# Issuing the natural K and V pair loads from GpSimd's software queue instead of SyncE's hardware queue, in an attention backward kernel

## The chip, the cores and the metric

The kernel runs on one core of a Trainium2 chip. The metric is the device time of one execution in microseconds (us). Runs are compared as fast runs of the same rounds on the same chip. "Same" means that the 95% interval of the ratio lies within 2%.

A ring is the list in memory through which one queue hands its transfers to the DMA engines. The engines are named as in the profile: PE (TensorE matmul) and PEld (its weight loads), DVE (VectorE), ACT (ScalarE), POOL (GpSimd) and SP (SyncE, which here only issues DMAs).

## The reference

The reference runs two independent blocks, A and B, of attention against a KV cache, and then takes the gradient of everything. The outputs are the forward result and ten gradients. Cut to what matters:

```python
# per block; B, Sq, D = 8, 96, 640;  H, Sk, Dh = 32, 512, 128;  bfloat16
q = (x @ wq).reshape(B, Sq, H, Dh).transpose(0, 2, 1, 3)
scores = jnp.einsum("bhqd,bhkd->bhqk", q, k_cache) * (Dh ** -0.5)
p = softmax(scores, axis=-1)
o = jnp.einsum("bhqk,bhkd->bhqd", p, v_cache)
out = o.transpose(0, 2, 1, 3).reshape(B, Sq, H * Dh) @ wo
# ... both blocks, then
_out, _vjp = jax.vjp(_f, A_x, A_k_cache, A_v_cache, A_wq, A_wo, B_x, B_k_cache, B_v_cache, B_wq, B_wo)
_grads = _vjp(grad_out)
```

K and V of one head and batch are 512 x 128 values each, 128 KB. Over two blocks, 32 heads and 8 batches that is 134 MB to read for both, and as much again in dK and dV to write.

## The kernel before

One head and batch is one *tick* of about 3.3 us; there are 512 ticks. The stages of a tick are spread over several ticks, so that PE works on different batches at once. The kernel's framework has a scheduler that orders each engine's instructions; what an engine gets is one list, and it works through that list in order.

The parts that matter here. K and V are loaded for two batches at a time (256 KB each, 256 runs of 1 KB), in rotating buffers:

```python
def c_ld(h, b):
    def f():
        K_sb = kvp.tile([128, 2, KC, 128], BF16, name="K_sb", bufs=7)
        V_sb = kvp.tile([128, 2, KC, 128], BF16, name="V_sb", bufs=5)
        nc.sync.dma_start(V_sb[:], vc[b:b + 2, h].rearrange("b (p c) d -> p b c d", c=KC))   # L233
        nc.sync.dma_start(K_sb[:], kc[b:b + 2, h].rearrange("b (p c) d -> p b c d", c=KC))   # L234
        # ... cut: the views are kept for later stages
    return f

def c_vt(h, b):      # V transposed by a DMA, issued on SyncE too
    def f():
        VT = kvp.tile([128, 2 * KC, 128], BF16, name="VT", bufs=4)
        nc.sync.dma_start_transpose(VT[:], CS[(blk, h, b)]["V2"][:].rearrange("p a c d -> p (a c d)"))  # L242
        # ... cut
```

POOL has two compute steps per tick. PE transposes the first one's result, and sums the second one's, later:

```python
# c_s3b: P = E / rowsum
P_sb = wk.tile([Sq, Sk], BF16, name="P_sb", bufs=5)
nc.gpsimd.tensor_scalar(P_sb[:], st["E_sb"][:], st["rinv"][:], 0.0, op0=ALU.mult, op1=ALU.add)   # L296
# c_s45, one tick later: PE transposes P_sb
nc.tensor.transpose(PT_ps[:, c * Sq:(c + 1) * Sq], P_sb[:, c * 128:(c + 1) * 128], ident[0:Sq, 0:Sq])   # L319
# c_s5b: O * dO, which PE sums into dl
nc.gpsimd.tensor_tensor(prod[:], hs["OT_h"][:, tok], hs["dOT_h"][:, tok], op=ALU.mult)   # L348
```

POOL's queue already issues other DMAs. The dK and dV stores stay on SyncE:

```python
nc.gpsimd.dma_start(wo_h[:], wo[h * 128:(h + 1) * 128, :])                 # L166, once a head
nc.gpsimd.dma_start(wq_h[:], wq_v[:, :, h * 128:(h + 1) * 128])            # L169, once a head
nc.gpsimd.dma_start(dwo[h * 128:(h + 1) * 128, :], dwo_sb[:])              # L435, once a head
nc.gpsimd.dma_start(wo_r[:, 0:groups[g], :], wo[...])                      # L463, once a group of heads, 1280 KB
nc.gpsimd.dma_start(tmp[:], src_flat[:, c * 128:(c + 1) * 128]...)         # L109, ld_tmp: block B's inputs, early
(nc.sync if first else nc.gpsimd).dma_start(t_[:], src_flat...)            # L136, x_nat and g_nat: SyncE in block A
nc.sync.dma_start(dv[b, h]..., dV_sb[:])                                   # L339, once a tick
nc.sync.dma_start(dk[b, h]..., dK_sb[:])                                   # L403, once a tick
```

## Time and profile before

| | before |
|---|---|
| time, median of 3 runs (range) | 1765.75 us (1764.09 to 1770.63) |
| span of the profiled run, granted clock | 1761.8 us, 1.0 |
| PE busy | 1727.7 us (98%) |
| POOL busy | 775.8 us (44%) |
| bytes moved, mean rate | 402 MB, 228 GB/s |

These are lines of the profile's page. The first gives the busy time of each engine, its share of the span and its instructions. Then come the DMA queues (q1 is the hardware queue, q0 the software queue; packets, MB, and the share of the sixteen DMA engines' time). Then one group of instructions per line: code line, engine, operation, names and shapes, count, busy time and mean ns of one, and after the second bar the engine's idle time before them with what ended most of it.

```profile
PE 1727.7 (98%) x24696; PEld 1467.1 (83%) x24696; DVE 1407.1 (80%) x3309; ACT 1426.4 (81%) x4041; POOL 775.8 (44%) x1378
...
DMA packets 578815, 402.15 MB, mean 228 GB/s; under 512 B 300512, under 2 KB 564192, under 8 KB 578496
...
q1 hardware_dynamic: 558624, 337.64, 80.0%
q0 software_dynamic: 19872, 60.32, 12.3%
...
L296 POOL TENSOR_SCALAR P_sb<-E_sb,rinv 96x512 bf16<-96x512 bf16 x512 | 352.1, 688 | 788.7 <-DVE rinv L287 785.5
```

PE is busy 98% of the span: it is the bound. POOL has more than half of its time free, and 785.5 us of that is one wait: before P_sb, for the reciprocal rinv that DVE delivers.

The list of waits of the same kernel gives engine, line and what it waited for, then us in total, times, and the longest. First over all engines, then for PE alone:

```profile
engine line waited for: us in total, times, longest us
POOL P_sb L296 <- DVE rinv L287: 785.5, 442, 3.7
```

```profile
PE tp_ps L127 <- DMA x_nat<-in_A_x_dram: 5.9, 1, 5.9
PE tp_ps L127 <- DMA g_nat<-in_grad_out_dram: 5.8, 1, 5.8
PE optp_ps L319 <- POOL P_sb L296: 2.6, 5, 1.2
```

PE waits for x_nat and g_nat at the start, once each. After that almost nothing holds it: POOL's P_sb delayed a transpose five times in 512 ticks. No K, V or VT landing is in PE's list.

Here is POOL's own timeline over two and a half ticks (start, duration, instruction, and in brackets the idle time before it and what ended it):

```profile
304.25 0.69 POOL L296 TENSOR_SCALAR P_sb<-E_sb,rinv 96x512 bf16<-96x512 bf16 x1 [2.43 <-DVE rinv L287]
304.91 0.36 POOL L348 TENSOR_TENSOR prod<-OT_h,dOT_h 128x96 bf16<-128x96 bf16 x1
307.42 0.69 POOL L296 TENSOR_SCALAR P_sb<-E_sb,rinv 96x512 bf16<-96x512 bf16 x1 [2.15 <-DVE rinv L287]
```

In a plain tick POOL works for one microsecond and stands for more than two. A load of 0.7 us fits into such a gap, if it comes at the right moment.

For the latencies that follow I matched every instruction of the trace with the one that uses its result. In this kernel K lands 16.15 us (median; 7.25 at the least) before its first transpose, VT 15.99 us (10.7 at the least) before the matmul dP that reads it, and P_sb ends 1.43 us (median; 1.25 at the fifth percentile) before its transposes start.

### The profile page before, as it was taken

Reading aid. Unit: us, or ns where it says so; the run is one execution under the profiler, and the core shown is the slowest. Engines: PE = TensorE matmul, PEld = TensorE weight load, DVE = VectorE, ACT = ScalarE, POOL = GpSimd, SP = SyncE. Lnnn points to the kernel's source line nnn. Section 1 sums busy time; section 2 is a strip of 40 time slices with the busy share of each in tenths; the row PEclk is TensorE's granted clock in tenths of the full one; section 3 lists DMA queues with packets and bytes.
Section 4 is the critical chain, followed back from the end, with each engine's and each line's share of the span. In section 5 each row is a group of like instructions: output and inputs, shape, how many; then the busy total and the mean of one; then the engine's idle time right before and its main releaser. Section 6 shows DMA issues by size and latency. Waiting matters only on the chain. (4 is left out here: it accounts for less than half of the span.)

```text
span 1761.8 us, 65690 instructions
## 1 busy us (share of the span) xinstructions
PE 1727.7 (98%) x24696; PEld 1467.1 (83%) x24696; DVE 1407.1 (80%) x3309; ACT 1426.4 (81%) x4041; POOL 775.8 (44%) x1378
## 2 busy tenths in 40 slices
PE   6999999999999999999999999999999999999998
PEld 5888888888888888888888888888888888888877
DVE  5888856888778887888878887678887888878884
ACT  4999977998679986798867998789976899768991
POOL 4444433444334443345465444344433444334445
PEclk9999999999999999999999999999999999999999
DMA  9999968999779997799999999789997899979982
GB/s 273 258 238 268 246 193 187 256 253 232 215 190 249 253 239 203 191 258 254 234 251 221 259 249 233 197 206 256 250 222 202 212 251 251 216 201 226 247 205 85
DMA packets 578815, 402.15 MB, mean 228 GB/s; under 512 B 300512, under 2 KB 564192, under 8 KB 578496
## 3 DMA queue, kind: packets, MB, share of 16 engines
q1 hardware_dynamic: 558624, 337.64, 80.0%
q0 software_dynamic: 19872, 60.32, 12.3%
q8 instruction: 193, 3.16, 0.8%
q14 instruction: 126, 1.03, 0.2%
HBM read 171.57 MB, written 159.12 MB: 188 GB/s over the span
## 5 line engine op out<-in xcount | busy, mean ns | idle before, releaser
L296 POOL TENSOR_SCALAR P_sb<-E_sb,rinv 96x512 bf16<-96x512 bf16 x512 | 352.1, 688 | 788.7 <-DVE rinv L287 785.5
L277 ACT ACTIVATE E_sb<-S_ps,negm 96x512 bf16<-96x512 f32 x512 | 348.5, 681 | 245.3 <-DVE negm L267 233.2
L362 DVE SCALAR_TENSOR_TENSOR dS_sb<-dP_ps,dl_ps,P_sb 96x512 bf16<-96x512 f32 x512 | 382.4, 747 | 110.2 <-PE dl_ps L360 106.4
L267 DVE TENSOR_REDUCE negm<-S_ps 96x1 f32<-96x512 f32 x512 | 347.4, 679 | 38.1 <-PE S_ps L265 32.7
L338 ACT ACTIVATE dV_sb<-dV_ps 128x512 bf16<-128x512 f32 x512 | 312.6, 611 | 0.5 <-DMA out_dram<-dV_sb 0.5
L402 ACT ACTIVATE dK_sb<-dK_ps 128x512 bf16<-128x512 f32 x512 | 300.3, 587 | 3.0 <-ACT dV_sb L338 2.0
L325 ACT ACTIVATE PT_sb<-optp_ps 128x384 bf16<-128x384 bf16 x512 | 253.5, 495 | 1.4 <-PE optp_ps L319 1.4
L254 DVE COPY KT<-kT_ps 128x512 bf16<-128x512 bf16 x512 | 212.6, 415 | 44.5 <-PE kT_ps L252 44.3
L336 PE MATMUL dV_ps<-dOnat_h,P_sb 96*128 96x128 bf16 x2048 | 197.9, 219 | 0.0
L252 PE MATMUL kT_ps<-ident,K_sb 128*128 128x128 bf16 x2048 | 197.9, 219 | 0.0
L400 PE MATMUL dK_ps<-Qnat_h,dS_sb 96*128 96x128 bf16 x2048 | 197.9, 219 | 0.0
L348 POOL TENSOR_TENSOR prod<-OT_h,dOT_h 128x96 bf16<-128x96 bf16 x512 | 185.9, 363 | 22.4 <-ACT OT_h L322 17.2
L265 PE MATMUL S_ps<-KT,QT_h 128*96 128x512 bf16 x512 | 193.8, 378 | 1.7 <-DVE KT L254 1.5
L358 PE MATMUL dP_ps<-VT,dOT_h 128*96 128x512 bf16 x512 | 195.2, 381 | 0.0
L385 DVE COPY dST_sb<-dq_dst_ps 128x384 bf16<-128x384 bf16 x512 | 178.0, 348 | 0.9 <-PE dq_dst_ps L383 0.8
L252 PEld LDWEIGHTS <-K_sb 128*128 128x128 bf16 x2048 | 147.2, 98 | 36.6 <-issue 1.6
L319 PE MATMUL optp_ps<-ident,P_sb 96*128 96x96 bf16 x2048 | 171.6, 205 | 2.8 <-POOL P_sb L296 2.6
L383 PE MATMUL dq_dst_ps<-ident,dS_sb 96*128 96x96 bf16 x2048 | 172.1, 206 | 1.6 <-DVE dS_sb L362 1.5
L312 PE MATMUL optp_ps<-PT_sb,V_sb 128*128 128x96 bf16 x2048 | 172.1, 206 | 0.0
L376 PE MATMUL dq_dst_ps<-dST_sb,K_sb 128*128 128x96 bf16 x2048 | 170.8, 206 | 0.3
L451 PE MATMUL dwq_ps<-dQnat,x_nat 128*128 128x128 bf16 x1920 | 143.2, 219 | 4.4
L431 PE MATMUL dwo_ps<-g_nat,Onat 128*128 128x128 bf16 (+1 forms) x768 | 140.5, 299 | 0.1
(82 smaller groups left out, 3698.7 us busy)
## 6 DMA issues: line engine op xcount, KB each, us to landing
out_dram<-dV_sb SPq DMA_DIRECT2D x512, 128.0 KB, 3.4
out_dram<-dK_sb SPq DMA_DIRECT2D x512, 128.0 KB, 3.5
V_sb<-in_A_v_cache_dram SPq DMA_DIRECT2D x128, 256.0 KB, 3.7
K_sb<-in_A_k_cache_dram SPq DMA_DIRECT2D x128, 256.0 KB, 4.0
K_sb<-in_B_k_cache_dram SPq DMA_DIRECT2D x128, 256.0 KB, 4.0
V_sb<-in_B_v_cache_dram SPq DMA_DIRECT2D x128, 256.0 KB, 3.6
out_dram<-dwq_sb POOLq DMA_DIRECT2D x64, 160.0 KB, 4.0
out_dram<-dwo_sb POOLq DMA_DIRECT2D x64, 160.0 KB, 3.9
```

The source lines that it names most:

```text
L252: nc.tensor.transpose(kT_ps[:, c * 128:(c + 1) * 128], st["K_sb"][:, c, :], ident[:])
L254: nc.vector.tensor_copy(KT[:], kT_ps[:])
L267: nc.vector.tensor_reduce(negm[:], S_ps[:], axis=AX.X, op=ALU.max, negate=True)
L277: nc.scalar.activation(E_sb[:], st["S_ps"][:], ACT.Exp, bias=st["negm"][:], scale=1.0, accum_out=rowsum[:])
L296: nc.gpsimd.tensor_scalar(P_sb[:], st["E_sb"][:], st["rinv"][:], 0.0, op0=ALU.mult, op1=ALU.add)
L325: nc.scalar.activation(PT_sb[:], PT_ps, ACT.Identity, scale=1.0)
L336: nc.tensor.matmul(dV_ps[:, c * 128:(c + 1) * 128], P_sb[:, c * 128:(c + 1) * 128], hs["dOnat_h"][:, b * 128:(b + 1) * 128], start=True, s ...
L338: nc.scalar.activation(dV_sb[:], dV_ps[:], ACT.Identity, scale=1.0)
L358: nc.tensor.matmul(dP_ps[:], hs["dOT_h"][:, tok], st["VT"], start=True, stop=True)
L362: nc.vector.scalar_tensor_tensor(dS_sb[:], dP_ps[:], dl_ps[:, 0:1], st["P_sb"][:], op0=ALU.subtract, op1=ALU.mult)
L400: nc.tensor.matmul(dK_ps[:, c * 128:(c + 1) * 128], dS_sb[:, c * 128:(c + 1) * 128], hs["Qnat_h"][:, b * 128:(b + 1) * 128], start=True, s ...
L402: nc.scalar.activation(dK_sb[:], dK_ps[:], ACT.Identity, scale=1.0)
```

## The change

The intent is to take 512 DMA issues off SyncE's queue, which also issues the V transposes and the dK and dV stores, and to put them on POOL's, which has idle time.

```diff
-            nc.sync.dma_start(V_sb[:], vc[b:b + 2, h].rearrange("b (p c) d -> p b c d", c=KC))
-            nc.sync.dma_start(K_sb[:], kc[b:b + 2, h].rearrange("b (p c) d -> p b c d", c=KC))
+            nc.gpsimd.dma_start(V_sb[:], vc[b:b + 2, h].rearrange("b (p c) d -> p b c d", c=KC))
+            nc.gpsimd.dma_start(K_sb[:], kc[b:b + 2, h].rearrange("b (p c) d -> p b c d", c=KC))
```

## The prediction

> **What bounds the kernel.** TensorE. The page has PE busy for 1727.7 of 1761.8 us (98%); most of the idle 30-odd us are two waits at the start (5.9 us for x_nat, 5.8 us for g_nat in the list of waits) and the ends. So freeing the SyncE queue cannot pay: no matmul waits for a K, V or VT landing in steady state. By the trace, matched instruction by instruction, K lands 16 us (median; 7 at worst) before its first transpose, VT 16 us (10.7 at worst) before dP.
>
> **What the change moves.** 512 loads (256 K, 256 V, 256 KB each) leave the SyncE queue, where each issue takes 0.39 us (200 us of 1762), for POOL, where a DMA is counted as work. POOL's own DMAs show the price: wo_h (128 runs of 1280 B) 0.60 us, wq_h (640 runs of 256 B) 0.91 us. A K or V load has 256 runs of 1 KB, so my estimate by interpolation is 0.68 us: 512 x 0.68 = 350 us, POOL 776 -> about 1125 us (64%). POOL has over 980 us of idle, 785 of it before P_sb, waiting for rinv.
>
> The Trainium skill (DMA: Bandwidth & Descriptors, "Issuing engines are not separate DMA queues") says all queues end on the same 16 engines, so I expect no bandwidth gain.
>
> **What lies on the critical path.** Only what delays P_sb (POOL) or prod (POOL), since PE transposes P one tick later. In the trace P_sb ends 1.25 us or more before its transposes in 95% of ticks (median 1.43), prod 1.43 us or more before dl. Loads are issued as soon as their buffer is released (K median 0.06, V 0.33 us after the last reader), each once in two ticks, about 0.8 us (V) and 1.3 us (K) before the next P_sb starts. Hence one load mostly fits in POOL's idle time; a collision costs P_sb at most about 0.7 us of its 1.25. Only double collisions (load plus the 0.91 us dwq or wq DMA) or an order in which POOL stands at the head of its queue waiting for a buffer release would reach PE. I allow 0 to 10 us for that.
>
> The Trainium skill (SBUF — State Buffer, "Who interferes with whom") warns that 2-port VectorE operations block descriptor writing. I expect none of it: here VectorE's large operations read PSUM, and POOL's present DMAs are steady (dwq_sb 0.86/0.92/0.93 us min/median/max).
>
> **Start-up.** g_nat lands at 12.45 us and PE waits for it. The first V and K loads stood behind it in the SyncE ring; now up to 1 MB more is in the other ring and may land before it: 1 MB at the 290 GB/s of the first 30 us is 3.6 us at most. I expect +2 us.
>
> **Sum.** 1765.75 + 2 (start) + 1.5 (collisions) = 1769 us; 8 in 10: 1759 to 1790. Faster over 2%: 0.02; within 2%: 0.86; slower over 2%: 0.12.
>
> **What would show it.** POOL busy 1080-1180 us, 0.6-0.75 us per load; PE busy unchanged within 5 us; the wait of PE/PEld for P_sb, 3.8 us before, below 15; K and VT still landing many us before use; PE's second start-up wait longer by 0 to 4 us.
>
> **What would make it wrong.** A per-load POOL time over 1.2 us; an in-order POOL queue that puts a load waiting for PE ahead of the P_sb that PE needs next (then 0.5 us or more per pair, over 100 us); a changed instruction order on PE.

## The result

| | before | after |
|---|---|---|
| time, median (range) of 4 runs | 1766.74 us (1764.09 to 1770.63) | 1765.84 us (1765.20 to 1766.98) |
| ratio, 95% interval | | 0.9994 (0.9974 to 1.0014): same |
| span of the profiled run, granted clock | 1761.8 us, 1.0 | 1764.3 us, 0.999 |
| after again, other rounds (last experiment) | 1768.16 us (1764.66 to 1771.70, 11 runs) | 1777.19 us (1771.11 to 1781.04, 4 runs), ratio 1.0048 (1.0024 to 1.0072): same |

A ratio here is the mean time of one kernel's fast runs over the mean of the other's in the same rounds, so it is not quite the ratio of the medians. The results were correct in every run told below.

The same lines of the page after the change, with one of the new groups of POOL:

```profile
PE 1721.9 (98%) x24547; PEld 1467.9 (83%) x24696; DVE 1407.6 (80%) x3309; ACT 1429.1 (81%) x4041; POOL 1151.6 (65%) x1890
...
DMA packets 480511, 402.15 MB, mean 228 GB/s; under 512 B 300512, under 2 KB 433120, under 8 KB 480192
...
q1 hardware_dynamic: 419360, 203.39, 54.6%
q0 software_dynamic: 60832, 194.57, 38.6%
...
L296 POOL TENSOR_SCALAR P_sb<-E_sb,rinv 96x512 bf16<-96x512 bf16 x512 | 356.5, 696 | 109.3 <-DVE rinv L287 77.8
...
L233 POOL DMA_DIRECT2D V_sb<-in_A_v_cache_dram x128 | 96.1, 751 | 106.5 <-PE optp_ps L319 105.7
```

POOL became 376 us busier, and the span did not follow. Its wait before P_sb for rinv fell from 785.5 to 77.8 us. The issue of one load costs POOL 0.75 us (0.70 to 0.795 over all 512). The bytes moved from q1 to q0: 134 MB, in 139264 packets fewer on q1 and 40960 more on q0. The Trainium skill ("DMA: Bandwidth & Descriptors", "Issuing engines are not separate DMA queues") says that DMAs of all issuing engines run on the same sixteen DMA engines, and that a second issuer saves only issue time. The equal mean rate of 228 GB/s is no test of that, since the same bytes in the same time give the same rate; that the two queues do share the engines is shown by the landings at the start, in experiments 7 to 10. (PE's count is lower after the change because 149 matmul records are missing from that trace; its busy time of 1721.9 is therefore a little too low.)

The waits of the changed kernel, over all engines and then for PE:

```profile
POOL V_sb L233 <- PE optp_ps L319: 211.1, 162, 3.4
POOL K_sb L234 <- PE dq_dst_ps L383: 138.9, 176, 2.5
```

```profile
PE tp_ps L127 <- DMA x_nat<-in_A_x_dram: 5.9, 1, 5.9
PE tp_ps L127 <- DMA g_nat<-in_grad_out_dram: 5.6, 1, 5.6
PE optp_ps L319 <- POOL P_sb L296: 2.9, 4, 1.4
```

POOL's idle time is now mostly in front of the loads: it stands at the head of its list until PE has read a buffer for the last time (211.1 us for V, 138.9 us for K). Yet PE waits for P_sb as little as before: 2.9 us in four places, against 2.6 in five. The timeline of POOL shows why:

```profile
303.36 0.36 POOL L348 TENSOR_TENSOR prod<-OT_h,dOT_h 128x96 bf16<-128x96 bf16 x1
305.06 0.76 POOL L233 DMA_DIRECT2D V_sb<-in_A_v_cache_dram  x1 [1.33 <-PE optp_ps L319]
305.86 0.70 POOL L296 TENSOR_SCALAR P_sb<-E_sb,rinv 96x512 bf16<-96x512 bf16 x1
306.52 0.37 POOL L348 TENSOR_TENSOR prod<-OT_h,dOT_h 128x96 bf16<-128x96 bf16 x1
307.71 0.76 POOL L234 DMA_DIRECT2D K_sb<-in_A_k_cache_dram  x1 [0.82 <-PE dq_dst_ps L383]
```

On average each tick now has one load (347 ticks have one, 75 have two, 88 none), and it lies in the gap before P_sb that used to be the wait for rinv. The matched latencies say the same. P_sb starts 0.47 us (median) after rinv instead of 0.10, and its slack before PE's transposes falls at the fifth percentile from 1.25 to 0.65 us. (The least is 0.06 us in both runs, at the places where PE did wait.) prod keeps 0.99 us (from 1.43) at the fifth percentile. K still lands 15.98 us before its use (9.91 at the least) and VT 15.93 us (10.8 at the least).

The totals hide one place. PE's wait before P_sb number 9 (counted from 0) grew from 0.39 us to 1.36 us. Two loads lie between that P_sb and the one before it; of the ticks with two loads it is the only one in which they held PE. Lines of POOL and the one of PE:

```profile
47.37 0.75 POOL L233 DMA_DIRECT2D V_sb<-in_A_v_cache_dram  x1 [0.64 <-PE optp_ps L319]
...
49.18 0.75 POOL L234 DMA_DIRECT2D K_sb<-in_A_k_cache_dram  x1
49.96 0.70 POOL L296 TENSOR_SCALAR P_sb<-E_sb,rinv 96x512 bf16<-96x512 bf16 x1
```

```profile
50.72 0.34 PE L319 MATMUL optp_ps<-ident,P_sb 96*128 96x96 bf16 x4 [1.36 <-POOL P_sb L296]
```

The same wait is 1.35 or 1.36 us in the profiled runs of experiments 7, 9, 10 and 12 and 1.09 us in 6, all with loads on POOL; it is 0.39 or 0.40 us in experiments 5 and 8, with the loads on SyncE. So one collision at the start does belong to the change. It costs under 1 us.

In the traces the order of PE's weight loads differs between the two kernels in two places near the start only, and so does that of DVE's instructions.

The end of the profiled run came 2.5 us later all the same. To see where, I took the time at which the k-th dK eviction on ACT ends, minus the same time in the run before:

| kernel, profiled run | k = 0 | 8 | 64 | 256 | 280 | 320 | 511 |
|---|---|---|---|---|---|---|---|
| after | -0.3 | 1.5 | 1.5 | 1.5 | 1.8 | 3.2 | 3.2 |
| after again (last experiment) | 0.4 | 10.6 | 10.6 | 10.6 | 18.1 | 18.1 | 18.2 |
| double POOL work (second experiment) | -1.1 | 2.6 | 12.5 | 31.5 | 33.4 | 39.4 | 57.6 |

The change costs nothing in the 248 ticks between k = 8 and k = 256, nor in the 191 after k = 320. A lag comes in the first eight ticks, where two waits for P_sb (0.85 us, and the one of 1.36 us above) make most of it in the first run, and once more in block B, which begins at k = 256: in the first run at k = 314 to 317, where PE waited 0.6 us for ACT's dK_sb, and in the repeat at k = 268. The size differs from run to run. The third row shows what a cost of the steady state would look like.

### The profile page after: what moved, and what is told of

Its sections match the earlier page's. It is cut to its first block, busy times and chain, and to the rows that moved or that the text cites. A ratio compares the mean times of both kernels' runs of the same rounds, so it can differ in the third digit from the quotient of the medians.

```text
span 1764.3 us, 65560 instructions
## 1 busy us (share of the span) xinstructions
PE 1721.9 (98%) x24547; PEld 1467.9 (83%) x24696; DVE 1407.6 (80%) x3309; ACT 1429.1 (81%) x4041; POOL 1151.6 (65%) x1890
## 5 line engine op out<-in xcount | busy, mean ns | idle before, releaser
L296 POOL TENSOR_SCALAR P_sb<-E_sb,rinv 96x512 bf16<-96x512 bf16 x512 | 356.5, 696 | 109.3 <-DVE rinv L287 77.8
L348 POOL TENSOR_TENSOR prod<-OT_h,dOT_h 128x96 bf16<-128x96 bf16 x512 | 187.8, 367 | 10.8 <-ACT OT_h L322 8.5
L233 POOL DMA_DIRECT2D V_sb<-in_B_v_cache_dram x128 | 96.3, 753 | 110.3 <-PE optp_ps L319 105.3
L233 POOL DMA_DIRECT2D V_sb<-in_A_v_cache_dram x128 | 96.1, 751 | 106.5 <-PE optp_ps L319 105.7
```

## The experiments

The main theory: POOL's idle time takes up all of the added work, and neither SyncE's relief nor the kind of queue is worth anything. The rivals: two real effects cancel (experiment 1); the room ends at a busy share of 100%, not earlier (2, 3, 11); the kind of queue matters by itself (4); the loads' long lead is what makes the change harmless (5, 6). Experiments 7 to 10 deal with the start, and 12 with the scatter. Experiments 1 to 4 shared rounds and one chip; so did 5 to 8, and 9 to 12.

### 1. The POOL work alone

Each load stays on SyncE, and POOL gets a memset of about the same length into the buffer before it.

```diff
-            nc.sync.dma_start(V_sb[:], ...)
-            nc.sync.dma_start(K_sb[:], ...)
+            nc.gpsimd.memset(V_sb[:, :, 0:3, :], 0.0); nc.sync.dma_start(V_sb[:], ...)
+            nc.gpsimd.memset(K_sb[:, :, 0:3, :], 0.0); nc.sync.dma_start(K_sb[:], ...)
```

> A POOL memset of three quarters of each K and V tile (768 elements a partition; my estimate from the 128-wide memset of 0.20 us and the 1-wide one of 0.10 us is 0.72 us) before each load; the loads stay on the SyncE queue. So POOL carries the same work and the same in-order waits for buffers as in the change, and the SyncE queue is not relieved. Theory (POOL's idle time before P_sb and P_sb's 1.25 us of room absorb it; relieving SyncE is worth nothing): POOL busy 1120 to 1180 us, time within 0.4% of before (1760 to 1773 us), PE waits for P_sb under 15 us. Rival (cost on POOL and gain on the SyncE queue cancel in the change): clearly slower than before, by 0.5% or more.

Measured: 1766.21 us (1765.58 to 1767.55) against 1767.47 us, ratio 0.9998 (0.9982 to 1.0015). The memset took 0.737 us, near a load's 0.748 (mean), and POOL was busy for 1137.3 us. PE's wait for P_sb was 2.6 us in four places. So 361 us of POOL work by itself cost next to nothing, and with it on POOL there is little gain of SyncE's relief left to look for: the change as a whole is at 0.9994. One thing makes this less than a clean test: the scheduler moved the wo_r and ld_tmp loads here too, and g_nat landed at 9.38 us instead of 12.45. In the profiled run that bought no time (the lag was 0.9 us at k = 0), but the start of this run is not that of the kernel before. From k = 8 to 511 its lag grew by 0.6 us, so in the steady state the cancellation of two larger effects falls.

### 2 and 3. Two and three times the POOL work

The change, with one such memset before each load, and then with two.

```diff
+            nc.gpsimd.memset(V_sb[:, :, 0:3, :], 0.0); nc.gpsimd.dma_start(V_sb[:], ...)
+            nc.gpsimd.memset(K_sb[:, :, 0:3, :], 0.0); nc.gpsimd.dma_start(K_sb[:], ...)
```

> The change plus one such memset before each load: about 1.45 us of POOL per load. Theory: POOL busy 1480 to 1560 us (about 85%), the room of P_sb mostly used up in ticks where load and memset meet, so PE begins to wait for P_sb: 0.5 to 4% slower than before (1775 to 1835 us). Rival (POOL has room as long as its busy share is below 100%): within 0.3% of before.

> The change plus two memsets before each load: about 2.2 us of POOL per load, POOL work about 1890 us, more than the whole span. Both theories: POOL bounds the kernel, 1900 to 2050 us, PE waits for P_sb over 100 us. It shows what the profile looks like when POOL does reach the chain.

Measured: 1821.48 us, ratio 1.0312 (1.029 to 1.0334), and 2068.13 us, ratio 1.1706 (1.1687 to 1.1725). Busy line of the page and PE's longest wait, first with one memset, then with two:

```profile
PE 1730.8 (95%) x24547; PEld 1470.7 (81%) x24696; DVE 1408.5 (77%) x3309; ACT 1432.6 (79%) x4041; POOL 1506.4 (83%) x2402
```

```profile
PE optp_ps L319 <- POOL P_sb L296: 49.4, 58, 1.9
```

```profile
PE 1796.7 (87%) x24547; PEld 1482.7 (72%) x24696; DVE 1418.1 (69%) x3309; ACT 1454.5 (70%) x4041; POOL 1863.7 (90%) x2914
```

```profile
PE optp_ps L319 <- POOL P_sb L296: 226.4, 273, 3.0
```

The doubled work came out as expected, the tripled work somewhat above. The room is used up at a busy share of 83%, well before 100%: PE waited 49.4 us for P_sb in 58 places. In the trace 37 of the 58 waits, with 36 us of the time, fall into a tick that comes once a head, in which POOL has, between two P_sb, the dwo store, prod, a K load, the wo_h load and a V load with its memset. What decides is how much stands between two P_sb in that one tick, not the mean share.

### 4. The loads on ACT's hardware queue

```diff
+            nc.scalar.dma_start(V_sb[:], ...)
+            nc.scalar.dma_start(K_sb[:], ...)
```

> The same loads on the ScalarE hardware queue instead: it relieves SyncE just as the change does, with the cheap 0.39 us issue, but on an engine busy 81% that stands in the loop S -> E -> P. Theory (what matters is how much room the queue's own engine has, in order, not which kind of queue): 200 us of issue plus waits for buffers against 335 us of idle: slower by 1 to 5% (1783 to 1855 us), with PE waiting for ScalarE results. Rival (the kind of queue matters, hardware is cheaper): same as before or better, 1755 to 1770 us.

Measured: 1781.30 us (1779.60 to 1782.70), ratio 1.0081 (1.006 to 1.0101): "same", yet a cost, and less than I had expected. PE's waits:

```profile
PE tp_ps L127 <- DMA g_nat<-in_grad_out_dram: 8.0, 1, 8.0
PE tp_ps L127 <- DMA x_nat<-in_A_x_dram: 7.4, 1, 7.4
PE optp_ps L312 <- ACT PT_sb L325: 6.0, 10, 0.8
```

PE waited 3.7 us longer in sum for x_nat and g_nat (8.0 and 7.4 us, against 5.8 and 5.9), and ACT's PT_sb held PE for 6.0 us in ten places; K was issued 7.2 us (median) after its buffer was free, because ACT was at other work. The order of instructions changed too (in the trace 156 of PE's 24696 weight loads and 891 of ACT's 4041 instructions stand at another place), so this run does not price ACT's queue cleanly. It shows only that a hardware queue is not better as such. That the engine behind the queue is what counts fits these waits, but is not shown by this run alone.

### 5 and 6. Less room for K

Before and after, with five K buffers in place of seven.

```diff
-            K_sb = kvp.tile([128, 2, KC, 128], BF16, name="K_sb", bufs=7)
+            K_sb = kvp.tile([128, 2, KC, 128], BF16, name="K_sb", bufs=5)
```

> The kernel before with 5 buffers of K instead of 7. K landed 16 us (median) before its first transpose with 7; two pairs fewer are about 13.4 us, so about 2.7 us should be left (in the fastest ticks near 0). Theory (landings had far more room than they need): time within 0.5% of before, K landing 1.5 to 4 us before use (median), PE waits for K under 10 us. Rival (the room is needed): over 1% slower.

> The change with 5 buffers of K. With the room nearly gone the queue should begin to matter: POOL issues a K load later (behind P_sb, prod or another DMA) by up to 1.4 us and the issue takes 0.75 instead of 0.39 us. Theory: 0 to 1.5% slower than before (1765 to 1792 us), and slower than the same kernel with the loads on SyncE (sent with it) by 0 to 20 us, PE waiting for kT's K loads. Rival (the queue never matters): equal to that kernel within 2 us.

Measured: with SyncE 1766.60 us, ratio 0.9997 (0.9978 to 1.0016). K then landed 4.27 us (median) before its use, instead of 16.15, a little more than I had expected. With POOL 1772.59 us (1766.29 to 1777.16), ratio 1.0026 (1.0002 to 1.0051); K landed 3.93 us (median) before its use, and in the profiled run PE waited for a K landing twice, 3.5 us in sum.

Some 12 of the 16 us of lead are spare for either queue. With the short lead, the POOL version shows a few late landings; but its time is no worse than that of the changed kernel with seven buffers in other rounds (1777.19), so I do not put its 0.3% down to the buffers.

### 7. A large load first in POOL's queue

In the changed kernel the scheduler had put block A's first wo_r load (1280 KB) at 23.07 us; before the change it was issued at 3.24 us. This experiment puts it at the head of POOL's list, ahead of the K and V loads.

```diff
-        em.add(cLg + OFF["s5"] - 2, SL_LOAD, gW(g))
+        em.add(tick0 - 12 if (blk == 0 and g == 0) else cLg + OFF["s5"] - 2, SL_LOAD, gW(g))
```

> The change with the first load of wo_r (1.28 MB) put at the head of POOL's queue, where it stood before the change too (in the change the scheduler moved it from 3.2 to 23 us). My prediction of +2 us at the start assumed that more bytes in the other ring delay g_nat. Theory (bytes in the other ring share the engines and delay g_nat): g_nat lands 2 to 5 us later than the 12.3 us of the change, PE's first work on it too, time +2 to +5 us over the change. Rival (the rings do not slow each other at the start): g_nat lands at 12 to 13 us and the time is that of the change.

Measured: 1767.83 us (1766.38 to 1777.34, 6 runs), ratio 1.0019 (0.9995 to 1.0043). g_nat landed at 14.01 us, against 12.28 after the change: later, but by 1.7 us and not by 2 to 5. The run also shows something I had not asked for. These are lines of POOL's timeline:

```profile
1.33 1.05 POOL L463 DMA_DIRECT2D wo_r<-in_A_wo_dram  x1 [0.39 <-issue]
...
11.82 0.72 POOL L234 DMA_DIRECT2D K_sb<-in_A_k_cache_dram  x1 [4.04 <-DMA wo_r<-in_A_wo_dram]
```

The ninth DMA of POOL's list waited 4.04 us for the first one to land, though the two have no tensor in common. In the changed kernel, where wo_r comes later, there is no such wait at this place. The trace shows the link: the DMAs of POOL's queue take eight semaphores (counters that tell of a landing) in turn, numbers 102 to 109, and not one of the 852 that have another eight places before them started before that one had landed. So each is held back until the one eight before it has landed, whatever tensor that one is for. This comes back in experiment 12.

### 8. A light start, without the change

The kernel before, with the early wo_r and ld_tmp loads held back. A one-column copy on POOL reads a tensor that comes later and so delays the load; the load then overwrites what it wrote. PE's order stays the same.

```diff
-                nc.gpsimd.dma_start(tmp[:], src_flat...)
+                nc.gpsimd.tensor_copy(tmp[:, 0, 0:1], HS[(0, 28)]["wqT_h"][:, 0:1]); nc.gpsimd.dma_start(tmp[:], src_flat...)
...
-            nc.gpsimd.dma_start(wo_r[...], wo[...])
+            (nc.gpsimd.tensor_copy(wo_r[:, 0, 0:1], HS[(blk, 0)]["wqT_h"][:, 0:1]) if blk == 0 and g == 0 else None); nc.gpsimd.dma_start(wo_r[...], wo[...])
```

> The kernel before, loads on SyncE, with wo_r's first load and the second block's ld_tmp loads held back (a one-column copy on POOL that reads a later tile) so that only wo_h and wq_h, 0.32 MB, share the engines with x_nat and g_nat. Theory: g_nat lands at about 8 us instead of 12.45 (2.3 MB at 290 GB/s), PE starts 3 to 5 us earlier, time 2 to 5 us under before (1761 to 1764 us). Rival: g_nat's landing stays at 12 us, and so does the time.

Measured: 1762.63 us (1761.33 to 1766.51, 6 runs), ratio 0.9975 (0.996 to 0.999). PE's wait for g_nat:

```profile
PE tp_ps L127 <- DMA g_nat<-in_grad_out_dram: 2.7, 1, 2.7
```

g_nat landed at 9.35 us instead of 12.45 (about 8 was expected), and PE waited 2.7 us for it instead of 5.8. The gain of 0.25% is within 2%, but its interval lies below 1. It is the only version whose interval lies wholly ahead of the kernel before, and it has nothing of the change in it.

### 9 and 10. A light start with the change

The change with the same two loads held back; then the same, with the K and V loads of block A's first two heads on SyncE.

```diff
+            (nc.sync if blk == 0 and h < 2 else nc.gpsimd).dma_start(V_sb[:], ...)
+            (nc.sync if blk == 0 and h < 2 else nc.gpsimd).dma_start(K_sb[:], ...)
```

> The change with the same two holds as the light start of the kernel before (first wo_r load and the second block's ld_tmp loads held back). POOL's queue now starts with wo_h, wq_h and three V and K pairs (1.8 MB). Theory (what delays g_nat is the bytes in the other ring, whichever tensor they belong to; in the change the pairs took the place of wo_r and ld_tmp, which is why my +2 us did not come): g_nat still lands at 11.5 to 12.8 us and the time is that of the change (within 2 us). Rival (it was wo_r alone): g_nat at about 9.4 us and 3 us less time.

> As the previous one, with the pairs of the first two heads left on SyncE, behind g_nat. Only wo_h and wq_h share the engines with x_nat and g_nat. Theory: g_nat at 9 to 10 us, time 2 to 4 us less than the change, level with the light start of the kernel before (within 2 us: POOL's later loads cost nothing). Rival: no gain.

Measured: 1774.91 us (1768.88 to 1785.31, 6 runs), ratio 1.0038 (1.0013 to 1.0064), and 1775.15 us (1766.71 to 1778.77, 6 runs), ratio 1.0037 (1.0015 to 1.0058).

The landings of g_nat agree with the theory, which was that the bytes in the *other* ring count, whichever tensor they are of:

| kernel | issued on POOL before g_nat's landing | of it moved by then | g_nat landed |
|---|---|---|---|
| 8 (SyncE, held back) and 10 | wo_h, wq_h: 320 KB | 320 KB | 9.35 us in both |
| before | wo_h, wq_h, wo_r, one ld_tmp: 1792 KB | 1663 KB | 12.45 us |
| after, and 9 | wo_h, wq_h, six K and V loads: 1856 KB | 1548 and 1584 KB | 12.28 and 12.42 us |
| 7 | wo_r, wo_h, wq_h, six K and V loads: 3136 KB | 2376 KB | 14.01 us |

The issued sizes are summed from those of the single issues, the moved ones from the trace's packets on q0. What counts is what has moved by then: in experiment 2, where memsets held the loads back, 1600 KB had been issued but only 852 KB moved, and g_nat landed at 10.35 us; in experiment 3 it was 832 and 548 KB, and 9.39 us. The Trainium skill ("DMA: Bandwidth & Descriptors", "Queues, rings and completion order") says that each DMA engine goes round-robin between the queue rows it has work for, packet by packet; the table agrees with that. Loads that stand behind g_nat in its own ring delay it less: in experiment 8 four of them, 1024 KB, were issued by 3.72 us, and 255 KB had moved when g_nat landed.

In time, experiment 10 missed. It won 3 us at the start, as meant (PE waited 2.65 us for g_nat in the profiled run), and was not clearly faster than experiment 9 or 12. The scatter of the versions with loads on POOL was larger than what was sought. On the time this pair is inconclusive.

### 11. Double POOL work, without the pile-up

Experiment 2, with the wo_h load and the dwo store moved to SyncE.

```diff
-            nc.gpsimd.dma_start(wo_h[:], wo[h * 128:(h + 1) * 128, :])
+            nc.sync.dma_start(wo_h[:], wo[h * 128:(h + 1) * 128, :])
...
-                nc.gpsimd.dma_start(dwo[h * 128:(h + 1) * 128, :], dwo_sb[:])
+                nc.sync.dma_start(dwo[h * 128:(h + 1) * 128, :], dwo_sb[:])
```

> The doubled POOL work (one memset per load, 1821 us) with only the wo_h load and the dwo_sb store taken off POOL, to SyncE: 128 DMAs of 0.6 us, about 77 us of POOL. In the trace of the doubled kernel 37 of the 58 stalls of PE for P_sb (36 of 50 us) stood in one tick a head, where dwo's store, prod, a K load, wo_h's load, the V memset and a V load all lie between two P_sb. Theory (a pile-up of POOL items in one tick costs, not POOL's total): stalls fall to under 25 and 20 us, time 1775 to 1800 us, with POOL still busy about 80%. Rival (the total work of POOL costs): about 1815 us, the stalls spread over other ticks.

Measured: 1796.88 us (1791.05 to 1812.72, 4 runs), ratio 1.0177 (1.0139 to 1.0214), unclear by the 2% rule. PE's waits:

```profile
PE S_ps L265 <- ACT dK_sb L402: 22.4, 16, 3.8
...
PE optp_ps L319 <- POOL P_sb L296: 5.6, 9, 1.2
```

POOL was still busy for 1438.3 us (79%), only 68 us less than in experiment 2, but PE's wait for P_sb fell from 49.4 us to 5.6 us. The tick concerned shows it best. From one S_ps matmul to the next it took 2.90 us before and after the change, 3.96 us in experiment 2 and again 2.90 us here (medians over the heads). The pile-up in one tick was the cause of those waits, not the busy share. The median time came down by 24.6 us and not by the full 44 us, and a new wait of 22.4 us is there: the dK stores left SyncE late (ACT waited 25.8 us for them), and PE waited for the bank of accumulator memory that ACT should have emptied. Experiments 2 and 11 ran on different chips, so the 24.6 us are rough. (The profiled run was the slowest of the four, so the new wait is at its largest here.)

### 12. The changed kernel again

No edit; the changed kernel in the rounds of experiments 9 to 11.

> The change itself again. In its first trace the lag behind the trace of before came in two places alone (1.8 us in the first eight ticks, 1.6 us at the change of block), nothing in between. If this lag belongs to the change it comes again in both places; if it is scatter, at least one is gone. Time 1763 to 1770 us, within 0.2% of before.

Measured: 1777.19 us (1771.11 to 1781.04), ratio 1.0048 (1.0024 to 1.0072). The expectation was missed: 11 us slower than the same kernel in its first rounds, while the kernel before moved by 1.4 us. The table of lags above shows where: 10 us in the first eight ticks and 7.5 us soon after the block switch, nothing in between. (The expectation's "1.6 us at the change of block" was read too coarsely: in the first trace that lag stands some fifty ticks later.)

Busy time by stretches of the profiled run (window; its us; then busy time and instructions of PE, PEld, DVE, ACT and POOL; then granted clock, DMA share, GB/s):

```profile
core 0: us, PE busy (x) PEld busy (x) DVE busy (x) ACT busy (x) POOL busy (x), PEclk, DMA share, GB/s
...
37.00:43.00 6.00, 0.34 (x7) 0.25 (x5) 0.00 (x0) 0.42 (x1) 0.82 (x1) 0.89 1.35 303
43.00:46.00 3.00, 2.77 (x12) 1.70 (x12) 1.16 (x3) 3.00 (x10) 1.26 (x3) 0.50 0.74 126
46.00:48.70 2.70, 2.70 (x32) 2.59 (x29) 1.61 (x5) 1.70 (x6) 2.56 (x4) 0.53 1.14 187
...
933.00:938.00 5.00, 0.11 (x2) 0.11 (x3) 0.95 (x4) 0.99 (x4) 1.59 (x3) 0.80 1.42 190
938.00:941.50 3.50, 3.50 (x32) 3.26 (x32) 1.44 (x3) 1.12 (x3) 3.44 (x7) 0.50 0.83 272
```

At 37.3 us PE stood for 5.9 us, at 933.0 us for 4.9 us. After each pause it ran at a granted clock of 0.5 (the rows with 0.50 and 0.53), from 41.7 to 48.5 and from 936.0 to 942.8 us, 6.8 us each time. The Trainium skill ("TensorE: Matmul & The Clock Gate", "Part 1: The HAM clock gate (the "warmup" mystery)") gives half rate as the default after an idle window, with windows of about 3.4 us. The lengths in the traces agree: 0.5 for 3.4 us in the first run of the changed kernel, and for twice that here. The idle window is there only in this run: in the first run the half clock, from 25.8 to 29.2 us, followed a stretch of 3.4 us in which PE was busy for 1.45 us, with no pause of over 1.5 us. So each pause costs PE a further 3.4 us of work (half of 6.8): 5.9 + 3.4 = 9.3 us of the 10.2 us of lag gained by k = 8, and 4.9 + 3.4 = 8.3 us against the 7.5 us after the switch.

What made the second pause? POOL's timeline, and PE's first instruction after it:

```profile
921.07 0.90 POOL L463 DMA_DIRECT2D wo_r<-in_B_wo_dram  x1
...
928.25 0.57 POOL L498 DMA_DIRECT2D out_dram<-ob  x1
936.37 0.73 POOL L234 DMA_DIRECT2D K_sb<-in_B_k_cache_dram  x1 [7.55 <-DMA wo_r<-in_B_wo_dram]
937.14 0.70 POOL L296 TENSOR_SCALAR P_sb<-E_sb,rinv 96x512 bf16<-96x512 bf16 x1
```

```profile
937.89 0.50 PE L319 MATMUL optp_ps<-ident,P_sb 96*128 96x96 bf16 x4 [4.94 <-POOL P_sb L296]
```

wo_r is issued at 921.07 us. The eighth DMA after it in POOL's list is a K load (the line at 928.25 is the seventh), and it waits 7.55 us until wo_r has landed. P_sb stands behind it in the list, so it starts at 937.14, and PE waits 4.94 us for it. The K load and wo_r carry the same semaphore in the trace, as eighth neighbours do (experiment 7).

In the first run of the changed kernel the same wait was there, but only 2.3 us long, and it did not hold PE: wo_r landed 10.3 us after its issue there, and 14.75 us after it here. In the kernel before no idle time of POOL is ended by another DMA in this way: it has 348 DMAs in POOL's list, not 860, and each began at least 2.2 us after the one eight before it had landed.

At the first pause PE was held by another engine. One V transpose on SyncE took 6.37 us to issue at 34.7 us, the dV store behind it was late, ACT waited 7.7 us for it before it could reuse dV_sb, and PE waited 5.9 us for ACT:

```profile
ACT dV_sb L338 <- DMA out_dram<-dV_sb: 7.7, 1, 7.7
...
PE dP_ps L358 <- ACT dV_sb L338: 5.9, 1, 5.9
...
POOL ld_tmp L109 <- DMA wo_r<-in_A_wo_dram: 5.6, 1, 5.6
```

Why that issue took so long, the trace does not say. But POOL's list stood at the same time for the reason of the second pause: its ld_tmp load waited 5.6 us for block A's wo_r, which landed 17.8 us after its issue, against 8.7 us in the first run. In both pauses, then, a large load was slow to land.

No run was made in which only these waits were taken away. That they make the lag of this run is read from its trace; how often they come, and whether the chip or the round decides it, stays open. What the runs as a whole show: the kernel before scattered from 1763.4 to 1771.8 us in 33 timed runs, while experiments 6, 7, 9, 10 and 12, all with loads on POOL, reached 1777 to 1785 us. Each of them is "same", but four of these five ratios (6, 9, 10 and 12: 1.0026 to 1.0048) have an interval wholly above 1, so a small cost is likely. Experiments 6 and 7 did so on another chip than 9, 10 and 12.

## Why the prediction was right

It predicted 1769 us and "within 2%" at 0.86. The median was 1765.84 us, and 1777.19 us in the repeat; both lie in the range of 1759 to 1790. That 1769 lies between the two medians is luck, as the last point tells. Point by point:

- **"So freeing the SyncE queue cannot pay."** Right. In neither kernel does a matmul wait for a K, V or VT landing, and experiment 1, with the loads left on SyncE, took about the same time as the change.
- **"POOL busy 1080-1180 us, 0.6-0.75 us per load."** Right, the second at its edge. The load cost 0.748 us on average, not the 0.68 of the estimate: it lies above the straight line, in the number of runs, between the two DMAs that I interpolated between. Why is not shown. POOL was busy for 1151.6 us, not for 1125.
- **"Only what delays P_sb (POOL) or prod (POOL)" counts, and the slack of 1.25 us takes up one load.** Right, and shown by three runs: 376 us of POOL work raised PE's waiting for P_sb by 0.3 us in sum, the double amount cost 49.4 us, and without the pile-up the double amount cost 5.6 us. It is a matter of what stands between two P_sb in one tick.
- **Collisions, +1.5 us.** Of about the right size, but not where it was looked for. The mechanism named was a double collision, of a load with a wq or dwq DMA. In the changed kernel 62 ticks after the first have a wq load and a K load ahead of P_sb, and none of them held PE. In the steady state this term was 0. What did collide were two loads, once, at P_sb number 9: PE's wait there was 1.36 us, not 0.39.
- **Start-up, +2 us.** It did not come: g_nat landed at 12.28 us, not later than at 12.45. The prediction missed that the scheduler would move wo_r and ld_tmp back when the loads came into POOL's list. As many bytes left the other ring as came in (experiments 7 to 10).
- **VectorE's two-port operations would not block descriptor writing.** Right so far as it can be seen: the Trainium skill ("SBUF — State Buffer", "Who interferes with whom") warns of it, and here the 512 loads took 0.70 to 0.795 us, with no long ones among them.
- **"PE busy unchanged within 5 us."** 1721.9 after 1727.7, with 149 records missing. The repeat lost none and had 1734.1, of which about 6.8 us are the two stretches at half clock.
- **What it left out.** It named "an in-order POOL queue that puts a load waiting for PE ahead of the P_sb that PE needs next". The loads do wait for PE, 350 us in all (211.1 and 138.9), and it is harmless, because PE has freed the buffer in time for P_sb. What does hold PE now and then is a load waiting for another *DMA*, after the block switch. That, the slow issue in the first ticks and the clock after each pause made most of the 18 us of lag in the profiled repeat; in the first run the lag was 3 us. The 1765.84 us of the first rounds show less of it than the 1777.19 of the repeat, and the two terms of +2 and +1.5 that I had added stand for a cost that came from elsewhere.

## What to carry to other kernels

Before you give an engine more DMAs to issue, look at what waits for its compute and at the slack of that step in the worst tick, not at its mean busy share: here 65% cost nothing in the steady state, 79% without a pile-up cost PE 5.6 us of waiting for that engine, and 83% with a pile-up in one tick of each head cost 3%. A queue that nothing waits on is not worth relieving. Where DMAs share an in-order list with compute, find out which earlier DMA each of them waits for: it can be one that has nothing to do with it.

## What the Trainium skill lacked or had wrong

- "DMA: Bandwidth & Descriptors" calls descriptor generation "small, variable". By these runs an issue keeps POOL for 0.60 us (128 runs of 1280 B), 0.75 us (256 runs of 1 KB) or 0.91 us (640 runs of 256 B). With 512 loads that is 376 us of its time with compute standing behind it.
- The same page says that a wait for a semaphore happens on the issuing sequencer, before the DMA is dispatched. Neither it nor "GPSIMD Engine Reference" says what that means for an engine that also computes: a K load at the head of POOL's list waited 7.55 us for another DMA, P_sb stood behind it, and PE lost 4.94 us.
- No page says that the queue's eight semaphores, as this program hands them out, tie each DMA to the one eight before it. Moving wo_r to the first place moved such a wait, of 4.04 us, to the ninth DMA.
- "DMA: Bandwidth & Descriptors", "Issuing engines are not separate DMA queues", says that spreading issues only saves time on the sequencer. At the start it also shifts who lands first, as its section on arbitration would let one expect: g_nat landed at 9.35, 12.28 to 12.45, and 14.01 us, when 320, 1548 to 1663, and 2376 KB had moved through the other ring.
- "TensorE: Matmul & The Clock Gate" gives half rate after an idle window of about 3.4 us, but not how idle a window has to be. In the first run of the changed kernel half rate followed 3.4 us in which PE was busy for 1.45 us, with no pause of over 1.5 us.
